# Layer 1 three segments behind layer 0 instead of four, in a two-layer recurrent-memory transformer

## The chip, the core and the metric

The kernel runs on one core of a Trainium2 chip. TensorE (PE, with its weight loads PEld) multiplies matrices into PSUM; VectorE (DVE) and ScalarE (ACT) read PSUM and do the element-wise work; GpSimd (POOL) works on SBUF only and issues some DMAs; SyncE (SP) issues most of them. The metric is the device time of one execution in microseconds, the median of the runs shown. The profile is one further execution.

## The reference

```python
def A(x, mem0, Wq, Wk, Wv, Wo):                 # x: 2048 x 512, 32 heads of 128
    mem = mem0                                  # 8 rows
    for s in range(64):                         # segments of 32 rows
        h = concat([mem, x[32*s:32*s+32]])      # 40 rows
        q, k, v = h @ Wq, h @ Wk, h @ Wv        # per head
        p = softmax(mask(q @ k.T * scale))
        o = (p @ v) @ Wo                        # summed over the heads
        mem = o[:8]; out[s] = o[8:]
B = lambda x: relu(x @ w1) @ w2                 # 512 -> 1376 -> 512
x = x + A(layernorm(x), ...);  x = x + B(layernorm(x))      # layer 0
x = x + A(layernorm(x), ...);  x = x + B(layernorm(x))      # layer 1, same weights
```

The recurrence is the memory: segment s needs the eight memory rows that segment s-1 has made. All weights stay in SBUF. Operands are bf16, sums and residual rows f32.

## The kernel before

**Steps.** Step k does segment k of layer 0 and, at the same time, segment k-4 of layer 1 (`DELTA = 4`; the segment of layer 1 done in step s has the name s). Steps 0 to 3 have only layer 0, steps 4 to 63 both, steps 64 to 67 only layer 1. Where both run, the 40 rows of each lie side by side in `HT` and are the 80 moving columns of one matmul per block of weights. A step's TensorE queue is written out by hand (as are those of VectorE, SP and GpSimd; ScalarE's is ordered by a scheduler when the program is built):

1. `qk` (L580 to L615): queries and keys of heads 0 to 15 into `qp`, evicted by ScalarE (`QT`) and VectorE (`KT`); then some filler; then `scores` into the banks `sp`. VectorE and ScalarE do the softmax of this half (`exponentials`, `softmax`; its products are on GpSimd, the last one of a step on VectorE), and a DMA transpose makes `PT0`.
2. The same for heads 16 to 31. The first dense product (`dense_h`, tile `hp`) lies ahead of the second scores. Filler follows while the softmax of the second half runs, then `transpose_p` on TensorE (tile `tp`), `weighted_v` (tile `pv`) and the copies `outputs`.
3. The hand-over of the memory: `output_mem` (tile `wo`), ScalarE's copy `wm`, the selection matmuls `mt`, the copies into `HT` and `HTm`, `memory_values` (tile `vm`). Then the next step.

**Filler** is what no step waits for: outputs of the previous step's token rows (`output_x`, tile `wox`), the dense layer (`dense_h`, `dense_y`), values of layer 0's later segments (`values0`, tile `vp`) and of layer 1's next segment (`values1`, tile `v`). Values go to DRAM and come back in a later step into `Vs`. `values1(k + 1)` fills the two waits of the hand-over, 16 matmuls each.

**Riding.** `output_mem` has stationary blocks of 32 columns: 16 are the memory rows of the two layers, 16 are spare. Token rows of segments k % 4 == 0 ride in the spare columns of two steps, layer 0's in steps k and k+1, layer 1's in k+2 and k+3 (`ride0`, `ride1`, `output_ride`, `add_ride`). The others go through `output_x` one step later, both layers' 64 rows as one block of width 64 (L373, two side by side in the array).

**Residual rows.** `residual(d)` is a 128 x 512 tile for two steps; a step has 64 rows, layer 0's 32 and layer 1's 32. Rows of d are normalized in step k = d + 2 (`prepare`, `normalize_step`; VectorE, with one `pow` on GpSimd), transposed by a DMA (`transpose_step`), used by `dense_h(k - 2)` and by `values1`, and summed by `dense_y` (L543, width 64) and `add_dense`. Layer 0's finished rows are copied to the place where layer 1 will add to them (L566).

**PSUM.** `ps_c` has three buffers (queries, keys, `mt`, `vm`), `ps_fill` two (`hp`, `v`, `vp`, `xp` and two of the `pv`), `ps_wo` one (`wo`, `wox`, a `vp`), and two banks hold the scores and, in turn, the dense sums.

Of the kernel before, what the change touches and what calls it, by code (L numbers as in the profile page):

```python
# [16 lines left out]
LN_EPS = 1e-5  # L17
DELTA = 4
# [4 lines left out]
def kernel(  # L23
# [23 lines left out]
    assert NSEG % 4 == 0 and DELTA == 4  # L47
    LAST = NSEG + DELTA - 1
    NXT = NSEG // 4
    NC4 = Dm // 128  # L50
    NFC = (Dff + 127) // 128
# [23 lines left out]
    def ride0(k):  # L75
        return has0(k) and k % 4 == 0

    def ride1(s):
        return has1(s) and s % 4 == 0 and s + DELTA <= LAST

    def place1(s):
        if ride1(s):
            return s + 4, 32
        if s >= LAST - 1:
            return LAST - 1, 32 * (s - LAST + 1)
        return s, (0 if s % 4 == 0 else 32)
# [6 lines left out]
    def base(d):  # L93
        return 64 * (d % 2)

    def span(d):
        offs = ([0] if has0(d) else []) + [o for o, _ in slots_of.get(d, [])]
        return base(d) + min(offs), base(d) + max(offs) + 32
# [11 lines left out]
    R_tiles = {}  # L110

    def residual(d):
        i = d // 2
        if i not in R_tiles:
            R_tiles[i] = wk.tile([128, Dm], F32, tag=f"R{i % 2}", bufs=3 - i % 2, name="R")
        return R_tiles[i]

    def load_x(k):
        r = base(k)
        nc.gpsimd.dma_start(out=residual(k)[r:r + SEG, :], in_=A_x[0, SEG * k:SEG * k + SEG, :])  # L120
# [41 lines left out]
    mhalf_t = const.tile([128, 1], F32)  # L162
# [30 lines left out]
    stats_all = const.tile([128, 6], F32)  # L193
    nc.vector.bn_stats(out=stats_all[:], in_=XN[:])
# [20 lines left out]
    xT0, xnT_tiles, hT_tiles, vd0, vd1, vmds, wm_tiles, wo_tiles, xp_tiles, vp_tiles, obs = {}, {}, {}, {}, {}, {}, {}, {}, {}, {}, {}  # L215

    def stat_tail(stats, of=""):
        mom = wk.tile([128, 3], F32, tag="ln_mv" + of, bufs=2 - len(of), name="mv")
# [3 lines left out]
        nc.gpsimd.tensor_tensor(out=rstd, in0=rstd, in1=mhalf_t[:], op=ALU.pow)  # L222
        return mv, rstd
# [11 lines left out]
    def moments_x(n):  # L235
        return stat_tail(stats_x(n), "x")
# [17 lines left out]
    def norm_parts(k):  # L254
        parts = []
        d = k - 2
        if 0 <= d <= LAST:
            parts.append((nc.vector, residual(d)) + span(d))
        if has1(k + 1):
            g = k + 1 - DELTA  # L260
            parts.append((nc.vector, residual(g), base(g), base(g) + SEG))
        return parts

    def moments(k, later):
        for _, R, lo, hi in norm_parts(k)[1:] if later else norm_parts(k)[:1]:
            nc.vector.bn_stats(out=stats_all[lo:hi, :], in_=R[lo:hi, :])

    norm_rows = {}

    def normalize_step(k):  # L270
        mom = stat_tail(stats_all) if norm_parts(k) else None
        masks(*layers(k))
        def rows():
            for eng, R, lo, hi in norm_parts(k):
                normalize(eng, XN, R, mom, lo, hi)


        if len(layers(k)) == 1 or k == DELTA:
            norm_rows[k] = rows
        else:  # L280
            rows()
# [4 lines left out]
    def transpose_step(k):  # L286
        if not norm_parts(k):
            return
        t = xnT_tiles[k] = wk.tile([128, NC4, 128], BF, tag="xnT", bufs=1, name="xnT")
        if k <= LAST:  # L290
            nc.sync.dma_start_transpose(out=t[:], in_=XN[:])
        else:
            tp = transpose_pe(XN)
            nc.scalar.copy(out=t[:], in_=tp[:])
# [3 lines left out]
    evict_behind = []  # L298

    def values0(p, n, lo=0, hi=NC4, pool=None, stage=None, late=False):  # L300
# [15 lines left out]
        if late and evict_behind:  # L316
            with tc.issue_after(evict_behind[0]):
                nc.scalar.copy(out=vst, in_=vp[:])
        else:
            nc.scalar.copy(out=vst, in_=vp[:])  # L320
# [15 lines left out]
    def values_second(ii, stage):  # L336
        if ii == 0:
            vd0[0] = dram.tile([2, 4, 32, 512], BF, tag="vd_second", bufs=1, name="vd_second")
        values_tile(xT0[0][:, :, SEG:2 * SEG], ii, vd0[0], stage)

    def values1(s, ii):
# [4 lines left out]
        r = base(s - DELTA)  # L346
        values_tile(xnT_tiles[s - 1][:, :, r:r + SEG], ii, vd1[s])

    def values_tile(tokens, ii, vd, stage=None):
        vp = ps_fill.tile([128, 512], F32, tag="fill", name="v1")  # L350
        for c4 in range(NC4):
            for j in range(4):
                n = 4 * ii + j
                nc.tensor.matmul(vp[32 * j:32 * j + 32, :], lhsT=tokens[:, c4, :],  # L354
# [3 lines left out]
        nc.scalar.copy(out=vst, in_=vp[:])  # L358
# [4 lines left out]
    def ox_span(k):  # L363
        offs = ([0] if has0(k) and not ride0(k) else [])
        if has1(k) and not ride1(k):
            offs.append(place1(k)[1])
        r = base(place1(k)[0] if k == LAST else k)
        return (r + min(offs), r + max(offs) + 32) if offs else None

    def halves(out, lhsT, rhs, start, stop):  # L370
        nr = lhsT.shape[-1]
        for j in range(2):
            nc.tensor.matmul(out[64 * j:64 * j + nr, 0:256], lhsT=lhsT, rhs=rhs[:, 256 * j:256 * j + 256],  # L373
                             start=start, stop=stop, tile_position=(0, 64 * j))

    def add_halves(dst, in0, half_sums):
        nr = in0.shape[0]
        for j in range(2):
            nc.vector.tensor_tensor(out=dst[:, 256 * j:256 * j + 256], in0=in0[:, 256 * j:256 * j + 256],
                                    in1=half_sums[64 * j:64 * j + nr, 0:256], op=ALU.add)  # L380

    def output_x(k, lo, hi):
        if not 0 <= k <= LAST or ox_span(k) is None:
            return
        r0, r1 = [x % 64 for x in (ox_span(k)[0], ox_span(k)[1] - 1)]
        r1 += 1
        if lo == 0:
            pool, tag = (ps_wo, "wo") if k < LAST else (ps_c, "c")
            wo_tiles[k] = pool.tile([128, Dm], F32, tag=tag, name="wox")
        for h in range(lo, hi):  # L390
            if r1 - r0 == 64:
                halves(wo_tiles[k], OTx[:, h, r0:r1], Wo_sb[:, h, :], h == 0, h == H - 1)
            elif by_heads(k):
                for j in range(2):
                    q = 32 * (2 * (h % 2) + j)
                    nc.tensor.matmul(wo_tiles[k][q:q + 32, 0:256], lhsT=OTx[:, h, r0:r1],  # L396
                                     rhs=Wo_sb[:, h, 256 * j:256 * j + 256], start=(h < 2), stop=(h >= H - 2),
                                     tile_position=(0, q))
            else:
                for j in range(4):  # L400
                    nc.tensor.matmul(wo_tiles[k][32 * j:32 * j + 32, 0:128], lhsT=OTx[:, h, r0:r1],
                                     rhs=Wo_sb[:, h, 128 * j:128 * j + 128], start=(h == 0), stop=(h == H - 1),
                                     tile_position=(0, 32 * j))

    def by_heads(k):
        return k == LAST or len(layers(k + 1)) == 1

    def add_last(k, part):

        r = 64 * (LAST - k)  # L410
        R = residual(LAST - 1)
        nc.vector.tensor_tensor(out=R[r:r + 64, 0:256], in0=R[r:r + 64, 0:256],
                                in1=wo_tiles[k][64 * part:64 * part + 64, 0:256], op=ALU.add)
# [3 lines left out]
    def last_rows(k, eng):  # L417
# [3 lines left out]
        R = residual(LAST - 1)  # L421
# [6 lines left out]
        nc.vector.bn_stats(out=stats[:, 0, :], in_=R[r:r + 64, 0:256])  # L428
# [5 lines left out]
        nc.gpsimd.tensor_tensor(out=rstd, in0=rstd, in1=mhalf_t[r:r + 64, :], op=ALU.pow)  # L434
        eng.tensor_scalar(out=XN[r:r + 64, 0:256], in0=R[r:r + 64, 0:256], scalar1=mv[:, 0:1], scalar2=rstd[:, 0:1],  # L435
                          op0=ALU.subtract, op1=ALU.mult)

    def turn_last(k, t, copy):
        r = 64 * (LAST - k)
        c = SEG * (LAST - k)  # L440
# [4 lines left out]
        copy(out=t[:, :, c:c + SEG].rearrange("p (j b) t -> p b j t", j=2),  # L445
             in_=tp[:].rearrange("p b (j t) -> p b j t", j=2))

    def add_output(k, part=None):
        if not 0 <= k <= LAST or ox_span(k) is None:
            return  # L450
        r0, r1 = ox_span(k)
        R = residual(k)
        if by_heads(k) and r1 - r0 == 32:
            for q in range(4):
                if part in (None, q // 2):
                    cs = slice(256 * (q % 2), 256 * (q % 2) + 256)
                    nc.vector.tensor_tensor(out=R[r0:r1, cs], in0=R[r0:r1, cs],
                                            in1=wo_tiles[k][32 * q:32 * q + 32, 0:256], op=ALU.add)
        elif part == 1:
            return  # L460
# [20 lines left out]
    def output_ride(k):  # L481
        if ride_rows(k) is None:
            return
# [667 lines left out]
```

## Time and profile before

| what | value |
|---|---|
| median of 3 runs | 1582.27 us (1580.9 to 1583.86) |
| span of the profiled execution | 1580.0 us |
| PE busy | 1548.6 us, 98%, 42866 matmuls |
| PEld busy | 1286.3 us, 81% |
| DVE busy | 1277.3 us, 81% |
| ACT busy | 734.7 us, 47% |
| POOL busy | 349.8 us, 22% |
| step 1 begins (first `qp` matmul) | 51.20 us |
| step 3 begins | 91.97 us |
| step 4, the first with both layers, begins | 111.66 us |
| step 64, the first with layer 1 alone, begins | 1495.70 us |

Matmuls are pipelined, and four or two of them run side by side where their stationary blocks are narrow, so the mean duration of one (200 ns for L591) is not what it costs; the distance from one group's start to the next one's is. The queue share of the page says that TensorE works nearly always; which group it works on, and what would stand behind it, is read from its timeline.

### The profile page before, as it was taken

The numbers are of one execution on the slowest core, as the hardware profiler recorded it, in microseconds if no ns is written. First come the engines' busy times: TensorE is split into PE (matmuls) and PEld (weight loads), VectorE is DVE, ScalarE is ACT, GpSimd is POOL, SyncE is SP. The second block draws the span as 40 slices with busy tenths as digits, with TensorE's granted clock in tenths as the row PEclk, the third lists the DMA queues.
The fourth block names the chain that finished last, engine by engine and source line by source line (L and its number), as shares of the span: only waits on it lengthen the run. The fifth ranks groups of instructions, "written<-read, shape, count | busy, mean of one in ns | idle before, by whom it ended". The sixth has DMA issues, their size and how long they took to land. (4 is left out here: it accounts for less than half of the span.)

```text
span 1580.0 us, 95139 instructions
## 1 busy us (share of the span) xinstructions
PE 1548.6 (98%) x42866; PEld 1286.3 (81%) x42866; DVE 1277.3 (81%) x3300; ACT 734.7 (47%) x1762; POOL 349.8 (22%) x670
## 2 busy tenths in 40 slices
PE   5899999999999999999999999999999999999998
PEld 3677888888888888888888888988888898888876
DVE  3578888888888888888888888888888888887866
ACT  3435445454544545454454545445454544545433
POOL 2012122222222222222122222212222221222110
PEclk9999999999999999999999999999999999999999
DMA  9734432434353244434433343443443344333331
GB/s 369 246 77 76 87 84 78 81 92 79 78 92 84 78 82 94 80 76 91 84 80 80 99 80 76 88 84 79 77 99 77 72 87 80 82 74 95 75 69 41
DMA packets 222021, 146.26 MB, mean 93 GB/s; under 512 B 123464, under 2 KB 215984, under 8 KB 221616
## 3 DMA queue, kind: packets, MB, share of 16 engines
q1 hardware_dynamic: 218448, 135.96, 38.8%
q8 instruction: 336, 5.51, 1.5%
q0 software_dynamic: 3072, 4.20, 1.1%
q14 instruction: 69, 0.57, 0.1%
q10 hardware_dynamic: 96, 0.03, 0.0%
HBM read 65.41 MB, written 45.35 MB: 70 GB/s over the span
## 5 line engine op out<-in xcount | busy, mean ns | idle before, releaser
L597 ACT CAST QT<-qp 128x480 bf16<-128x480 f32 (+3 forms) x408 | 201.5, 494 | 433.4 <-PE qp L591 433.1
L591 PE MATMUL qp<-HT,Wq_sb 128*128 128x80 bf16 (+1 forms) x8704 | 371.3, 200 | 3.2 <-POOL HT L786 1.2
L591 PEld LDWEIGHTS <-Wq_sb 128*128 128x128 bf16 x8704 | 325.9, 100 | 35.2 <-issue 27.5
L591 PE MATMUL qp<-HT,Wk_sb 128*128 128x80 bf16 (+1 forms) x8704 | 347.3, 199 | 1.7 <-issue 1.3
L591 PEld LDWEIGHTS <-Wk_sb 128*128 128x128 bf16 x8704 | 319.5, 100 | 2.6 <-issue 1.6
L664 POOL TENSOR_TENSOR P_sb<-es,sm 128x320 bf16<-128x320 f32 x185 | 130.8, 721 | 714.8 <-ACT QT L597 299.4
L599 DVE CAST KT<-qp 128x480 bf16<-128x480 f32 (+3 forms) x408 | 220.3, 565 | 36.3 <-PE qp L591 32.9
L643 DVE TENSOR_REDUCE mx<-sp 128x8 f32<-128x320 f32 x256 | 115.1, 487 | 133.1 <-PE sp L625 130.9
L373 PE MATMUL wox<-Wo_sb,OTx 128*64 128x256 bf16 x2880 | 173.6, 273 | 0.0
L373 PEld LDWEIGHTS <-OTx 128*64 128x64 bf16 x2880 | 150.2, 110 | 2.9
L649 ACT ACTIVATE es<-es 128x320 f32<-128x320 f32 x256 | 109.5, 468 | 61.9 <-DVE es L647 61.0
L797 PE MATMUL vm<-Wv_sb,HTm 128*32 128x512 bf16 x2176 | 129.4, 379 | 1.8 <-DVE KT L599 1.0
L354 PE MATMUL v<-Wv_sb,xnT 128*32 128x512 bf16 x2048 | 128.8, 378 | 0.0
L633 PE MATMUL wo<-Wo_sb,OTm 128*32 128x512 bf16 x2144 | 128.6, 380 | 0.0
L659 DVE TENSOR_REDUCE sm<-es 128x8 f32<-128x320 f32 x256 | 117.4, 459 | 13.5 <-ACT es L649 5.0
L617 DVE CAST sp<-maskb 128x320 f32<-128x320 bf16 x256 | 118.3, 483 | 0.0
L647 DVE TENSOR_TENSOR es<-sp,mx 128x320 f32<-128x320 f32 x256 | 113.6, 482 | 1.5
L543 PE MATMUL sp<-w_sb,hT 128*64 128x256 bf16 (+4 forms) x1452 | 103.9, 276 | 0.4 <-issue 0.4
L522 PE MATMUL hp<-xnT,w_sb 128*128 128x64 bf16 (+1 forms) x2948 | 98.5, 192 | 0.9 <-issue 0.5
L801 ACT CAST VmS<-vm 128x512 bf16<-128x512 f32 x134 | 78.5, 586 | 44.4 <-PE vm L797 42.5
L222 POOL TENSOR_TENSOR mv<-mv,mhalf_t 128x1 f32<-128x1 f32 x82 | 45.8, 558 | 224.6 <-DVE mv L221 218.9
L797 PEld LDWEIGHTS <-HTm 128*32 128x32 bf16 x2176 | 54.7, 97 | 48.8 <-issue 3.1
(125 smaller groups left out, 2088.5 us busy)
## 6 DMA issues: line engine op xcount, KB each, us to landing
Vs<-vd SPq DMA_DIRECT2D x96, 256.0 KB
vd<-vst SPq DMA_DIRECT2D x181, 128.0 KB
vmd<-VmS SPq DMA_DIRECT2D x134, 128.0 KB
Vs<-vmd SPq DMA_DIRECT2D x254, 32.0 KB
Vs<-vmd SPq DMA_DIRECT2D x60, 128.0 KB
Wq_sb<-in_A_Wq_dram SPq DMA_DIRECT2D x2, 2048.0 KB
Wk_sb<-in_A_Wk_dram SPq DMA_DIRECT2D x2, 2048.0 KB
Wv_sb<-in_A_Wv_dram SPq DMA_DIRECT2D x2, 2048.0 KB
```

The source lines that it names most:

```text
L354: nc.tensor.matmul(vp[32 * j:32 * j + 32, :], lhsT=tokens[:, c4, :], rhs=Wv_sb[:, c4, n * 512:(n + 1) * 512], start=(c4 == 0), stop=(c4 == ...
L373: nc.tensor.matmul(out[64 * j:64 * j + nr, 0:256], lhsT=lhsT, rhs=rhs[:, 256 * j:256 * j + 256], start=start, stop=stop, tile_position=(0, ...
L591: nc.tensor.matmul(qp[:, hi, 0:ncol], lhsT=W_sb[:, c4, h * Dh:(h + 1) * Dh], rhs=HT[:, c4, a_lo:a_hi, :], start=(c4 == 0), stop=(c4 == NC4 ...
L597: nc.scalar.copy(out=dst[:, 0:nh, a_lo * L:a_hi * L], in_=qp[:, 0:nh, 0:ncol])
L599: nc.vector.tensor_copy(out=dst[:, 0:nh, a_lo * L:a_hi * L], in_=qp[:, 0:nh, 0:ncol])
L617: nc.vector.tensor_copy(out=sp_tiles[a], in_=maskb2)
L633: nc.tensor.matmul(wo[32 * j:32 * j + 32, :], lhsT=OTm[:, h, n, 2 * M * c:2 * M * c + 4 * M], rhs=Wo_sb[:, h, :], start=(h < 4), stop=(h > ...
L643: nc.vector.tensor_reduce(out=mxs[a][:], in_=sp, axis=AX.X, op=ALU.max)
L647: nc.vector.tensor_tensor(out=es[:], in0=sp, in1=mxs[a][:].unsqueeze(2).to_broadcast([128, 8, L]), op=ALU.subtract)
L659: nc.vector.tensor_reduce(out=sm[:], in_=es[:], axis=AX.X, op=ALU.add)
L664: eng.tensor_tensor(out=P, in0=es[:], in1=sm[:].unsqueeze(2).to_broadcast([128, 8, L]), op=ALU.mult)
L797: nc.tensor.matmul(vp[32 * j:32 * j + 32, :], lhsT=HTm[:, c4, :], rhs=Wv_sb[:, c4, n * 512:(n + 1) * 512], start=(c4 == 0), stop=(c4 == NC ...
```

## The change

Layer 1 runs three segments behind layer 0. Steps 0 to 2 are layer 0 alone, 3 to 63 both, 64 to 66 layer 1 alone: 67 steps in place of 68. For this, layer 0's rows have to be finished a step earlier:

- Layer 0's outputs are made in their own step, in the hand-over (`output_own`, called in `new_memory` and `make_room`), where `values1` stood; `values1(k + 1)` moves ahead of them, into the second half's filler.
- Layer 0 doesn't ride. Every second segment of layer 1 does (`s % 2 == 0`); the others are `output_late`, 32 rows in the step behind. Every output block has width 32, four side by side.
- Residual rows lie by column halves: 64 partitions by 256 columns for a segment, so that each add or statistic takes half as many columns on twice the partitions. The halves' statistics are exchanged by four small copies, and `dense_y` has blocks of width 32. Loads and stores of such rows are two DMAs in place of one.
- The dense layer of d is done in step d + 1 in place of d + 2. The rows are normalized behind the first key copy of the step (`norm_rows`, `behind[0]`).
- Layer 0's value groups: 0, 1 or 2 in odd steps (48 over the 29 odd steps from 5 to 61), in place of 3 or 4 in every fourth.

```diff
-DELTA = 4
+DELTA = 3
...
     def ride1(s):
-        return has1(s) and s % 4 == 0 and s + DELTA <= LAST
+        return has1(s) and s % 2 == 0 and s + 4 <= LAST
...
+    def output_rows(t, a, lo, hi):
+        for h in range(lo, hi):
+            for j in range(2):
+                q = 32 * (2 * (h % 2) + j)
+                nc.tensor.matmul(t[q:q + 32, 0:HALF], lhsT=OTx[:, h, SEG * a:SEG * a + SEG],
+                                 rhs=Wo_sb[:, h, HALF * j:HALF * j + HALF], start=(h < 2), stop=(h >= H - 2),
+                                 tile_position=(0, q))
+    def output_own(k, lo, hi):
+        if lo == 0:
+            own_tiles[k] = ps_fill.tile([128, Dm], F32, tag="fill", name="own")
+        output_rows(own_tiles[k], 0, lo, hi)
...
     def dense_y
-            for j in range(2):
+            for q in range(2 * slots(d)):
+                o, j = divmod(q, 2)
-                nc.tensor.matmul(sp_banks[bank][64 * j:64 * j + n, 0:w], lhsT=hT_tiles[d][0:fs, fc, 0:n],
+                nc.tensor.matmul(sp_banks[1][32 * q:32 * q + 32, 0:w], lhsT=hT_tiles[d][0:fs, fc, SEG * o:SEG * o + SEG],
...
     def new_memory(k, cont, wo):
         nc.scalar.copy(out=wm_sb[:], in_=wo[:])
-        values1(k + 1, 0)
+        if has0(k):
+            output_own(k, 0, H // 2)
+        else:
+            values1(k + 1, 0)
...
     def prepare(k):
         moments(k, True)
+        add_own(k - 1)
         add_ride(k - 1)
         moments(k, False)
         normalize_step(k)
+    def make_room(k):
+        if has0(k):
+            output_own(k, H // 2, H)
+        else:
+            values1(k + 1, 1)
+        output_ride(k)
...
     def step(k):
+        first = 4 if k == LAST else 8 if single else 10
+        output_late(k, 0, first)
+        value_group(k, 0, 0, 2)
...
+        if k != LAST and not (single and has0(k)):
+            dense_h(d)
         with tc.high_priority(offset=PRIO):
             scores(qks, act)
             softmax(1, act, by_pe)
+        evict_behind.append(last_exp[0].ins)
+        value_group(k, 0, 2, NC4)
+        if single and has0(k):
+            value_group(k, 1, late=True)
+            dense_h(d)
...
+        if has0(k) and has1(k + 1):
+            values1(k + 1, 0)
+        output_late(k, second, H)
+        if not (single and has0(k)):
+            value_group(k, 1, late=True)
+        value_group(k, 2, late=True)
+        if has0(k) and has1(k + 1):
+            values1(k + 1, 1, late=True)
+        evict_behind.clear()
+            dense_y(d, 0, f_mid)
+            add_late(k)
```

An eviction with `late` is issued by ScalarE behind the last exponential of the step; one without has the place that the scheduler gives it.

More of the change, by code (lines that the diff above doesn't have):

```diff
@@ L315, in values0 @@
         vst = wk.tile([128, 512], BF, tag="vst", bufs=5, name="vst")[:] if stage is None else stage
[L316 to L320, printed above, removed]
+        evict(vst, vp[:], late)
         nc.sync.dma_start(out=vd0[p][n // 2].rearrange("j t e -> (j t) e"), in_=vst)
@@ L357, in values_tile @@
         vst = wk.tile([128, 512], BF, tag="vst", bufs=5, name="vst")[:] if stage is None else stage
-        nc.scalar.copy(out=vst, in_=vp[:])
+        evict(vst, vp[:], late)
         nc.sync.dma_start(out=vd[ii].rearrange("j t e -> (j t) e"), in_=vst)
[L363 to L368, printed above, removed]
```

521 lines of the change are left out of this document (200 added, 321 removed).

## The prediction

> **What bounds the kernel now.** I read the page's shares first (PE busy 98% of the span, DVE 81%, ACT 47%), then the busy time of each engine step by step. A step begins where the first `qp` matmul of a segment starts. The columns are: the stretch, its length, then busy time and instructions of PE, PEld, DVE, ACT, POOL, granted clock, DMA share, GB/s.
>
> ```profile
> 91.97:111.66 19.69, 19.08 (x582) 14.69 (x579) 14.70 (x38) 7.55 (x19) 3.71 (x8) 1.00 0.29 74
> 780.93:803.46 22.53, 22.53 (x611) 17.85 (x607) 19.20 (x51) 12.06 (x28) 5.66 (x11) 1.00 0.52 100
> 826.54:849.62 23.08, 23.08 (x650) 19.81 (x647) 19.56 (x51) 10.59 (x25) 5.34 (x10) 1.00 0.37 82
> ```
>
> A step with both layers lasts 23.08 us (22.53 in those that carry three groups of layer 0's values instead of outputs), and TensorE is busy throughout at full clock. A step with one layer lasts 19.69, nearly as long. The 60 two-layer steps run from 111.66 to 1495.70, 1384.0 us; four one-layer steps stand ahead and four (84.3 us) behind. So I price TensorE's queue from the start of one group to the start of the next, in the timeline of one step (start, us, count at the end):
>
> ```profile
> 836.89 1.45 PE L522 MATMUL hp<-xnT,w_sb 128*128 128x64 bf16 x44
> 838.27 0.57 PE L625 MATMUL sp<-KT,QT 128*40 128x40 bf16 x32
> 838.69 3.12 PE L373 MATMUL wox<-Wo_sb,OTx 128*64 128x256 bf16 x54
> 841.64 1.18 PE L543 MATMUL sp<-w_sb,hT 128*64 128x320 bf16 x18
> 842.65 0.45 PE L675 MATMUL tp<-ident,P_sb 128*64 128x80 bf16 x16
> 842.93 0.39 PE L543 MATMUL sp<-w_sb,hT 128*64 128x256 bf16 x4
> ...
> 844.16 1.91 PE L633 MATMUL wo<-Wo_sb,OTm 128*32 128x512 bf16 x32
> 845.90 1.04 PE L354 MATMUL v<-Wv_sb,xnT 128*32 128x512 bf16 x16
> 846.76 0.27 PE L857 MATMUL mt<-sel,wm 128*32 128x16 bf16 x16
> 846.87 1.03 PE L354 MATMUL v<-Wv_sb,xnT 128*32 128x512 bf16 x16
> 847.73 0.23 PE L488 MATMUL xp<-wm,sel 128*32 128x128 bf16 x4
> 847.79 1.90 PE L797 MATMUL vm<-Wv_sb,HTm 128*32 128x512 bf16 x32
> 849.62 0.57 PE L591 MATMUL qp<-HT,Wq_sb 128*128 128x80 bf16 x11
> ```
>
> The number behind the star is the width of the stationary block. `wo` and `vm` are the same 32 matmuls of width 32 on 512 columns. `wo`, followed by width 32, takes 845.90 - 844.16 = 1.74; `vm`, followed by width 128, takes 1.83. So **a change of width costs about 0.1 us**. The same in one-layer steps, where the dense rows are 32 wide:
>
> ```profile
> 102.40 1.06 PE L396 MATMUL wox<-Wo_sb,OTx 128*32 128x256 bf16 x32
> 103.28 1.18 PE L543 MATMUL sp<-w_sb,hT 128*32 128x320 bf16 x18
> 104.58 0.48 PE L675 MATMUL tp<-ident,P_sb 128*64 128x80 bf16 x16
> 104.99 0.40 PE L543 MATMUL sp<-w_sb,hT 128*32 128x256 bf16 x4
> ```
>
> Here `tp` to `sp` (64 to 32) takes 0.41, against 0.28 above (64 to 64). `wox` x32 of width 32 takes 0.88, and x16 followed by width 64 takes 0.55 (99.70 to 100.25), which is half of 0.88 plus 0.11.
>
> Last, the wait that the filler in mid-step has to cover. The score matmuls start at 838.27, and VectorE ends the last probabilities at 842.48:
>
> ```profile
> 838.69 0.89 DVE L643 TENSOR_REDUCE mx<-sp 128x8 f32<-128x320 f32 x2 [1.26 <-PE sp L625]
> ...
> 841.86 0.62 DVE L664 TENSOR_TENSOR P_sb<-es,sm 128x320 bf16<-128x320 f32 x1
> ```
>
> That is 4.21 after the scores began. With 0.1 for the hand-over `tp` could start at 4.31, and TensorE arrives at 4.38 (842.65). The kernel has no slack there.
>
> **The change, part by part.**
>
> *One step fewer.* The built program has 61 two-layer steps (3 to 63) and 67 in all. By forms this removes 512 `qp` matmuls of 40 columns at about 26 ns (13.4 us) and adds 256 of 80 columns at 36 (9.2); 32 `wo` and 32 `vm` go (3.6), and one two-layer step's `sp` and `pv` replace two one-layer ones' (1.2). That is 9 us less matmul work. Matmuls of width 64 on 256 columns become twice as many of width 32, four side by side: `wox` x32 at 0.88 is 27.5 ns each, half the 54.6 of L373, so this alone is worth nothing.
>
> *An even step (layer 1's outputs late).* Base 23.08.
> - Outputs: own 32 + 32 at 0.88 each, late 20 (5 fours: 0.55 + 0.11) and 44 (1.21): 3.63, against 0.57 + 2.95 before: +0.11. Layer 1's two value groups (0.86 each) only move from the step's end to its middle.
> - Dense sums: 36 + 8 of width 32 instead of 18 + 4 of width 64: +0.02 in length, +0.10 into `tp`, +0.10 behind it.
> - Scores (width 64) are now followed by width 32: +0.09 (0.50 for the 32 at 123.52, 0.42 here).
>
> Sum 23.50. `tp` is reached 0.51 + 0.86 + 1.21 + 0.86 + 1.13 = 4.57 after the scores. But ScalarE's order, as built, puts the eviction of the first value group (0.59) between its two exponentials. The group is finished about 1.6 after the scores, the first exponential starts at 1.74, so the second starts at 2.63 instead of 2.14, and VectorE's second sum, which had 0.2 to spare, comes 0.29 late: `tp` at 4.60. Wait 0.03, say 0.05: **23.55**, 30 times.
>
> *An odd step with two groups of layer 0's values.* No late outputs. Half a group in place of `wox` x10: 0.46 for 0.57. In the middle: half group 0.55, values 0.97, group 0.98, values 0.86 (three more changes of width, 64 to 32 and back) = 3.37 for 2.95. With 0.06 more in own and dense lengths and 0.2 at `tp`: 23.65. The second value group needs the PSUM buffer of the first (two `fill` buffers), whose eviction ScalarE puts behind both exponentials: 2.57 to 3.16 after the scores, while TensorE is there at 2.93. Wait 0.3: **23.95**, 19 times.
>
> *An odd step with one group.* Middle 2.28, so 22.56, and `tp` is reached 0.42 + 2.28 + 1.13 = 3.83 after the scores, 0.5 before it can start: **23.06**, 10 times, and step 3 likewise. Step 63 has no group: 21.6 and a wait of 1.0, **22.6**.
>
> *Sum of the two-layer steps.* 706.5 + 455.1 + 230.6 + 23.1 + 22.6 = 1437.9. Before, 12 x 22.53 + 48 x 23.1 = 1379.2, and the rest of its 1384.0 (4.9) was pauses marked "issue"; I add 5: **1443**.
>
> *Start.* Step 3 began at 91.97. Own outputs of steps 0 to 2 add 5.3; a second dense stage 2.7; values for step 3, 1.7; step 2's `wox` goes (2.0). Five gaps at the memory hand-overs (0.69, 0.47, 0.73, 0.34, 0.42) are filled by the own outputs: -2.6. The first dense stage is now in step 1, reached at about 64.4, and its weights are issued at 60.2: 1.41 MB at the 305 GB/s of 61 to 66 land near 66.3, the second 1.4 MB near 70. Waits of 2 and 0.6, less the 0.6 that TensorE spent there for the probabilities. Step 3 begins at **99** (97 to 103).
>
> *End.* The last three steps took 64.2; with the dense changes of width **64.8**.
>
> *What lies beside other work.* VectorE's chain ahead of the next step gains own sums (2 x 0.42) and four copies (0.16), loses two of the four 0.28 ride sums and half of each statistic (0.42 for 0.69), and the normalisation goes behind the first key copy. That copy starts 2.2 after the step's start, by these rows, against 2.64 now; the later ones 0.1 later, with 0.5 to spare before the scores. The normalised rows are ready at 3.7 instead of 2.6, so SP issues the transpose 1.1 later (1.2 us, then four loads of memory rows, needed only at 16.7); `hp`, which needs it, is at 10.3. Its landing shows in no row; the larger `PT` transpose took 5.84, so I bound this one by 0 and 5.84 from the issue and take no wait. A wait per us of lateness would cost 61 us. POOL has a second load to issue (0.59) where it sits idle 3.8, SP a second store (0.34) where it idles 0.1 to 1 between its issues; the two stores of layer 1's values (0.4 each) leave the step's end for its middle, where SP has nothing to issue from 839.6 to 848; own sums for VectorE's `OTx` copies: ready at 18.9 and 19.2 in the step, used at 19.7 and 20.7. I take 0.
>
> **Sum:** 99 + 1443 + 64.8 = 1606.8, against the profiled 1580.0: +27. The median of the runs is 2.3 above the profile, so I say **1609**.
>
> Changes of width make the sign: four more in an even step, five or three in an odd one, 251 in all, 24 us at 0.095. [...]
>
> **Rivals.**
> - *The changes of width are free and the fillers cover the chain* (faster). Then only the matmuls count: 24 and about 16 of waits less, 1569. For it: the trace has no idle time in these steps. Against it: each pair of rows above. The point from which it decides is 27 us saved of these 40, so a change of width at nearly 0. Chance 0.05.
> - *The changes cost as shown, but the waits vanish* (two PSUM buffers and ScalarE's order do not bind): 1593. For it: each wait is a difference of two sums, 0.03 to 0.9. Chance 0.13.
> - *The transpose comes late.* `hp` is 10.3 after the step's start and the issue at 3.9 to 5.1; it decides from a landing 5.2 after the issue ends. At 5.84 the price is 0.64 x 61 = 39: 1648. Against it: half of `PT`'s bytes. Chance 0.07.
> - *The forecast*, 0.75: own range 1598 to 1620.
>
> The range goes from 1593 (no waits) to 1625 (the waits twice as long): 0.85 of the chance. What can be told from no change is about 0.2%, 3 us. Faster 0.05, same 0.02, slower 0.93.
>
> **What would show it.** Two-layer steps of 23.5 (even) and 23.95 or 23.06 (odd); `sp` to `tp` gaps on PE ended by DVE's `P_sb` in odd steps with one group, and `v` ended by ScalarE's `vst` in those with two; a gap before the first `hp` near 64; a pause of 0.1 at each change of width. Wrong would be two-layer steps at or under 23.1, or idle time before `hp` in all of them.

## The result, and the profile after

| kernel | median | runs | span of the profiled execution |
|---|---|---|---|
| before | 1582.47 us | 1580.9 to 1583.86 (4) | 1580.0 us |
| changed | 1618.21 us | 1617.2 to 1621.24 (4) | 1616.0 us |

The ratio is 1.0229, 95% interval 1.0215 to 1.0244: slower by 36 us, of which 27 were forecast. An undisturbed step, here and below, is one of the shortest length that steps of its kind take again and again. The page of the changed kernel (span, shares of the engines, the queues of GpSimd's transfers and of the instruction fetches):

```profile
span 1616.0 us, 103053 instructions
...
PE 1568.8 (97%) x46705; PEld 1273.1 (79%) x46706; DVE 1229.6 (76%) x3463; ACT 728.4 (45%) x1708; POOL 365.4 (23%) x733
...
q0 software_dynamic: 6144, 4.20, 1.8%
q8 instruction: 366, 6.00, 1.6%
```

VectorE's busy time fell by 48 us and ScalarE's by 6. TensorE's rose by 20, with 3839 more matmuls, and TensorE is the engine that sets the time (busy for 97% of the span; 85% of the chain that ended last is its). The three kinds of two-layer step, in the busy time of each engine by stretch (length, then PE, PEld, DVE, ACT, POOL, clock, DMA share, GB/s):

```profile
741.11:764.66 23.55, 23.55 (x737) 19.71 (x733) 19.09 (x54) 10.54 (x25) 5.55 (x11) 1.00 0.32 76
764.66:788.56 23.90, 23.75 (x688) 18.84 (x685) 18.31 (x53) 11.69 (x27) 5.55 (x11) 1.00 0.45 91
812.10:835.24 23.14, 22.65 (x680) 18.40 (x677) 18.85 (x55) 11.05 (x26) 5.89 (x12) 1.00 0.37 83
```

An even step, an odd one with two groups of layer 0's values, an odd one with one: 23.55, 23.90 and 23.14, where 23.55, 23.95 and 23.06 were forecast. The middle of the even step on TensorE:

```profile
752.94 0.58 PE L573 MATMUL sp<-KT,QT 128*40 128x40 bf16 x32
753.45 1.05 PE L357 MATMUL v<-Wv_sb,xnT 128*32 128x512 bf16 x16
754.32 1.37 PE L371 MATMUL wox<-Wo_sb,OTx 128*32 128x256 bf16 x44
755.52 1.04 PE L357 MATMUL v<-Wv_sb,xnT 128*32 128x512 bf16 x16
756.39 1.18 PE L498 MATMUL sp<-w_sb,hT 128*32 128x320 bf16 x36
757.53 0.48 PE L623 MATMUL tp<-ident,P_sb 128*64 128x80 bf16 x16
757.94 0.40 PE L498 MATMUL sp<-w_sb,hT 128*32 128x256 bf16 x8
```

No idle time; `tp` to `sp` is 0.41, as in the old one-layer steps, where it was 0.28 in the old two-layer ones. In an odd step with one group the probabilities come too late for `tp`; the profile names the last thing VectorE did ahead of `tp` (L219), which ended 0.1 behind the probabilities:

```profile
826.45 1.18 PE L498 MATMUL sp<-w_sb,hT 128*32 128x320 bf16 x36
828.12 0.48 PE L623 MATMUL tp<-ident,P_sb 128*64 128x80 bf16 x16 [0.49 <-DVE mv L219]
```

The waits of all two-layer steps (101.19 to 1546.64; total us, times, longest) are few. These are the four largest of eight; the view leaves out idle times up to 0.15 us, and so 12 of the 19 waits ahead of `v` for its buffer:

```profile
PE tp L623 <- DVE P_sb L612: 3.6, 6, 1.2
PE tp L623 <- DVE mv L219: 2.4, 5, 0.5
PE qp L539 <- issue: 1.9, 4, 0.7
PE v L357 <- ACT vst L306: 1.1, 7, 0.2
```

From the starts of the steps the 36 us divide so:

| part | before | changed | difference | forecast, changed |
|---|---|---|---|---|
| up to step 3 | 91.97 | 101.19 | +9.2 | 99 |
| steps with both layers (before: with steps 3 and 64) | 1423.8 | 1445.5 | +21.7 | 1443 |
| the last three steps and the end | 64.2 | 69.4 | +5.2 | 64.8 |

The 1423.8 is 19.69 + 1384.0 + 84.3 - 64.2, so that both columns hold the same work: 61 steps of 23.70 in place of 60 of 23.07 and two of 20.

### The profile page after: what moved, and what is told of

It reads as the page before. It is cut to its first block, busy times and chain, and to the rows that moved or that the text cites. A ratio compares the mean times of both kernels' runs of the same rounds, so it can differ in the third digit from the quotient of the medians.

```text
span 1616.0 us, 103053 instructions
## 1 busy us (share of the span) xinstructions
PE 1568.8 (97%) x46705; PEld 1273.1 (79%) x46706; DVE 1229.6 (76%) x3463; ACT 728.4 (45%) x1708; POOL 365.4 (23%) x733
## 3 DMA queue, kind: packets, MB, share of 16 engines
q0 software_dynamic: 6144, 4.20, 1.8%
## 4 chain that ended last, share of the span: by engine, by line
PE 85%; DVE 3%; issue 2%; ACT 2%; POOL 0%; POOLq 0%; ACTq 0%
PE qp L539 36%; PE wo L581 7%; PE vm L724 7%; PE own L371 7%; PE hp L482 5%; PE v L357 5%; PE sp L498 4%; PE wox L371 4%; PE sp L573 3%; PE pv L649 3%; PE tp L623 2%; DVE es L595 1%; PE vp L318 1%; ACT es L597 1%; ACT vst L306 1%
## 5 line engine op out<-in xcount | busy, mean ns | idle before, releaser
L539 PE MATMUL qp<-HT,Wq_sb 128*128 128x80 bf16 (+1 forms) x8576 | 367.3, 200 | 1.8 <-POOL HT L710 1.2
L371 PEld LDWEIGHTS <-OTx 128*32 128x32 bf16 x6272 | 161.3, 96 | 26.0 <-issue 2.9
L371 PE MATMUL own<-Wo_sb,OTx 128*32 128x256 bf16 x4096 | 131.5, 272 | 0.5 <-issue 0.3
L728 ACT CAST VmS<-vm 128x512 bf16<-128x512 f32 x132 | 77.2, 585 | 103.5 <-PE vm L724 103.5
L276 POOL TENSOR_TENSOR mv<-mv,mhalf_t 128x2 f32<-128x2 f32 (+1 forms) x66 | 46.5, 705 | 295.8 <-DVE mv L275 261.5
L498 PE MATMUL sp<-w_sb,hT 128*32 128x256 bf16 (+1 forms) x2772 | 104.8, 276 | 0.8 <-DMA w_sb<-in_B_w_dram 0.5
L482 PEld LDWEIGHTS <-w_sb 128*128 128x128 bf16 x2948 | 90.3, 98 | 7.2 <-DMA w_sb<-in_B_w_dram 5.6
```

The source lines that it names most:

```text
L371: nc.tensor.matmul(t[q:q + 32, 0:HALF], lhsT=OTx[:, h, SEG * a:SEG * a + SEG], rhs=Wo_sb[:, h, HALF * j:HALF * j + HALF], start=(h < 2), s ...
L482: nc.tensor.matmul(hp[:, fc - f0, 0:n].rearrange("p (s t) -> p s t", s=ns), lhsT=w1_sb[:, c4, u:u + 128], rhs=cols(c4), start=(c4 == 0), s ...
L498: nc.tensor.matmul(sp_banks[1][32 * q:32 * q + 32, 0:w], lhsT=hT_tiles[d][0:fs, fc, SEG * o:SEG * o + SEG], rhs=w2_flat[0:fs, fc * Dm + HA ...
L539: nc.tensor.matmul(qp[:, hi, 0:ncol], lhsT=W_sb[:, c4, h * Dh:(h + 1) * Dh], rhs=HT[:, c4, a_lo:a_hi, :], start=(c4 == 0), stop=(c4 == NC4 ...
```

## The experiments

All ratios are to the kernel before.

**1. Only the dense sums narrow, in the kernel before.**

```diff
-            for j in range(2):
+            for q in range(2 * (n // 32)):
+                j, o = divmod(q, n // 32)
+                p = 64 * j + 32 * o
-                nc.tensor.matmul(sp_banks[bank][64 * j:64 * j + n, 0:w], lhsT=hT_tiles[d][0:fs, fc, 0:n],
+                nc.tensor.matmul(sp_banks[bank][p:p + 32, 0:w], lhsT=hT_tiles[d][0:fs, fc, 32 * o:32 * o + 32],
...
-                                 tile_position=(0, 64 * j))
+                                 tile_position=(0, p))
```

> The kernel before, with the dense sums of a two-layer step as four matmuls of width 32 side by side for each chunk and matrix instead of two of width 64 (44 matmuls instead of 22, the same sums). Everything else stays. Theory (a change of the stationary block's width costs about 0.095 us, the number of matmuls nothing): three more changes in each of 60 two-layer steps (64 to 32 ahead of the sums, 32 to 64 into the transposes, 64 to 32 behind them), 0.02 for the length of the sums: steps of 23.4 instead of 23.08, 18 us in all, a median near 1601; the gap from the start of the transposes to the start of the sums behind them grows from 0.28 to about 0.41. Rival (the change of width is free, and it is waits that cost time in the changed kernel): 1582 to 1584, steps of 23.1. Second rival (twice as many matmuls cost more by themselves): the sums x36 take clearly more than the 1.01 of x18, and the gap at the transposes stays 0.28.

Measured: 1602.33 us, ratio 1.0124 (1.0108 to 1.0139), +19.9 us. Steps of 23.43, and 22.80 in those with three value groups (22.53 before). Its timeline in step 35:

```profile
847.58 3.12 PE L373 MATMUL wox<-Wo_sb,OTx 128*64 128x256 bf16 x54
850.62 1.19 PE L543 MATMUL sp<-w_sb,hT 128*32 128x320 bf16 x36
851.75 0.48 PE L675 MATMUL tp<-ident,P_sb 128*64 128x80 bf16 x16
852.16 0.40 PE L543 MATMUL sp<-w_sb,hT 128*32 128x256 bf16 x8
```

`wox` x54 reaches the next group in 3.04 (2.95 where width 64 follows), the sums take 1.13 with the change into `tp` (1.01), `tp` 0.41 (0.28): 0.09, 0.12 and 0.13, in a kernel whose order and waits are the old ones. (23.43 - 23.08 - 0.02) / 3 is 0.11 for each change. Doubling the matmuls cost next to nothing by itself here: less 0.11 for the change into `tp`, the 36 sums take 1.02, and the 18 took 1.01.

**2. Layer 1's outputs narrow as well, in the kernel before.** To the edit above comes:

```diff
-        for j in range(2):
-            nc.tensor.matmul(out[64 * j:64 * j + nr, 0:256], lhsT=lhsT, rhs=rhs[:, 256 * j:256 * j + 256],
-                             start=start, stop=stop, tile_position=(0, 64 * j))
+        for q in range(4):
+            j, o = divmod(q, 2)
+            nc.tensor.matmul(out[32 * q:32 * q + 32, 0:256], lhsT=lhsT[:, 32 * o:32 * o + 32],
+                             rhs=rhs[:, 256 * j:256 * j + 256],
+                             start=start, stop=stop, tile_position=(0, 32 * q))
```

> As the first run, and layer 1's outputs too are four matmuls of width 32 side by side instead of two of width 64, still in layer 0's and layer 1's common tile and at their old places; four segments of distance, transposes, loads and waits as before the change. Theory (changes of width): in the steps that carry outputs a fourth change (width 32 ahead of and behind the first outputs and behind the scores, none any more between outputs and sums): 23.5, as in an even step of the changed kernel; in the 12 steps with three value groups as the first run, 22.85; in all 23 to 24 us, a median near 1606, which is most of the changed kernel's loss without any of its order. Rival (the loss comes from the new order: waits and late transposes): 1582 to 1586. A kernel at 1600 to 1603 would say that the outputs' changes cost less than those of the sums.

Measured: 1630.49 us, ratio 1.0302 (1.0282 to 1.0323), +48 us: twice what was expected. Undisturbed steps last 23.51 to 23.55, just as expected and just as the changed kernel's even ones. But 29 of the 44 two-layer steps that carry these outputs are longer, by up to 2 us. One of them, and the four largest of the nine waits of the two-layer steps (113.08 to 1545.76):

```profile
791.47 1.93 PE L374 MATMUL wox<-Wo_sb,OTx 128*32 128x256 bf16 x64
794.43 1.38 PE L374 MATMUL wox<-Wo_sb,OTx 128*32 128x256 bf16 x44 [1.02 <-issue]
```

```profile
PE wo L635 <- issue: 4.4, 7, 0.8
PE qp L593 <- issue: 4.0, 10, 0.7
PE wox L374 <- issue: 2.5, 5, 1.0
PE pv L703 <- issue: 2.3, 5, 0.9
```

TensorE stops in the middle of a row of equal matmuls whose data has long been there. The page counts 369 transfers on the instruction queue for 47,065 matmuls (336 for 42,866 before, 366 for 46,705 in the changed kernel): one fetch of 16,384 bytes for 127.5 matmuls. Pauses that follow each other directly are 125 to 128 matmuls apart, and each of the 49 in these steps ends 1.0 to 2.1 us behind the end of such a fetch. From the trace's DMA records and TensorE's matmul count, around the two pauses of step 34:

```
fetch from 839.48 to 841.36 us;   pause ends at 842.88, matmul 23,793
fetch from 844.37 to 845.41 us;   pause ends at 847.02, matmul 23,920
```

The profile puts the second of them down to `OTx`; its place, 127 matmuls behind the first and 1.6 us behind a fetch, is that of the others. That TensorE was out of instructions there is my reading: the records show the fetches and the stops, not what joins them. The fastest tenth of all stretches of 128 matmuls took at most 3.30 us here, 3.61 in the changed kernel, 3.93 in the one before. Taken as 12 undisturbed steps of 22.80 and 48 of 23.52, the two-layer steps would take 1402.6 us, 23.4 more than before without pauses (1379.2), which is the price of the changes; they took 1432.7, so that pauses are some 30 us.

**3 and 4. Changes of width added to the changed kernel, with a control.** Two matmuls of 16 columns among the second half of the own outputs, of width 64 or of width 32; their result goes to columns that nothing reads.

```diff
-        output_rows(own_tiles[k], 0, lo, hi)
+        t = own_tiles[k]
+        cuts = (lo, hi) if lo == 0 else (lo, 20, 28, hi)
+        for c0, c1 in zip(cuts, cuts[1:]):
+            if c0 > lo:
+                nc.tensor.matmul(t[0:64, 256:272], lhsT=ident[:, 0:64], rhs=ident[:, 0:16], start=True, stop=True,
+                                 skip_group_check=True, tile_position=(0, 0))
+            output_rows(t, 0, c0, c1)
```

> The changed kernel with two added matmuls of 16 columns and width 64 among the second half of each segment's own outputs (after heads 20 and 28; their result goes to unused columns), 64 steps. Theory (changes of width): four more changes a step, 64 x 4 x 0.095 = 24 us, and the matmuls themselves 1 to 3: a median near 1644. Rival (a change of width is free; it was the number of groups or waits): as the next run, within 2 us.

> The control of the run before: the same two matmuls of 16 columns at the same places, but of width 32, so that no width changes. Theory (changes of width): 1 to 4 us over the changed kernel, 1619 to 1622; the difference to the run before, 24 us, is the price of 256 changes of width. Rival (any added matmul between the others costs as much): as the run before.

Measured: 1651.74 us (ratio 1.0439, 1.0421 to 1.0456) with width 64, 1624.80 (1.0269, 1.0254 to 1.0284) with width 32. The second half of the own outputs in each, width 64 first:

```profile
827.39 0.39 PE L371 MATMUL own<-Wo_sb,OTx 128*32 128x256 bf16 x8
827.71 0.20 PE L402 MATMUL own<-ident 128*64 128x16 bf16 x1
827.83 0.62 PE L371 MATMUL own<-Wo_sb,OTx 128*32 128x256 bf16 x16
```

```profile
814.76 0.39 PE L371 MATMUL own<-Wo_sb,OTx 128*32 128x256 bf16 x8
814.98 0.17 PE L402 MATMUL own<-ident 128*32 128x16 bf16 x1
814.99 0.71 PE L371 MATMUL own<-Wo_sb,OTx 128*32 128x256 bf16 x19
```

The eight matmuls ahead last 0.32 or 0.22 from start to start, the small one 0.12 or 0.01: a tenth of a microsecond each way, and nothing where the width stays. Undisturbed even steps are 24.03 and 23.58 (23.55 without), odd ones 24.39 and 23.94: 0.45 for four changes, **0.11 each**. The medians differ by 26.9 us for 256 changes, 0.105 each. The control cost 6.6 us, more than the 1 to 4 expected: 0.04 a step is 2.6, and steps that are longer than undisturbed ones make up the rest; waits marked issue rose from 3.0 to 4.6 us in the two-layer steps.

**5. The kernel of run 2 with the same changes of width, but wide in the middle: fewer instructions, more changes.** In the kernel of run 2, `halves` takes the width from a flag:

```diff
-        for q in range(4):
-            j, o = divmod(q, 2)
+        n = 32 if narrow else 64
+        for q in range(128 // n):
+            j, o = divmod(q, 64 // n)
...
-                halves(wo_tiles[k], OTx[:, h, r0:r1], Wo_sb[:, h, :], h == 0, h == H - 1)
+                halves(wo_tiles[k], OTx[:, h, r0:r1], Wo_sb[:, h, :], h == 0, h == H - 1, h < 7 or h >= H - 2)
```

> The second run with 23 of layer 1's 27 heads in the long stretch at width 64 again; the four heads at its two ends and the five early heads stay at width 32. Per step that is 46 matmuls fewer and two changes of width more. Theory (code supply: the pauses marked issue, 24 us in the second run, come where 128 matmuls, which is one fetch of 16 KB of instructions, take less than about 3.8 us; they follow the number of instructions): most pauses go, 2 to 6 us of them stay, and two changes in 48 steps cost 9 us: 1606 + 9 + 2 to 6, a median of 1614 to 1621, faster than the second run in spite of more changes of width; undisturbed steps 23.7. Rival (the pauses are part of the price of narrow matmuls or of the changes): 1636 to 1645, undisturbed steps of 23.7 and as many pauses or more.

Measured: 1615.23 us, ratio 1.0213 (1.0198 to 1.0228): 15 us faster than run 2 with two more changes a step. Undisturbed steps are 23.75, so these two cost 0.12 each. The waits of its two-layer steps, whole list:

```profile
PE qp L593 <- issue: 1.1, 3, 0.4
PE wox L403 <- issue: 0.7, 1, 0.7
```

So the pauses of run 2 don't go with the changes of width: with two more of them a step, the two-layer steps took some 3 us more than undisturbed ones, and in run 2 some 30. Run 5 has fewer matmuls in that stretch and, by the same edit, fewer narrow blocks; against the blocks speaks the changed kernel, where every output block is 32 wide and pauses are 7.5 us. The 3.8 us of the expectation is an estimate between the 3.61 of the changed kernel and the 3.93 of the one before; no run shows a limit there.

**6. One load of the residual rows per segment.**

```diff
-        for j in range(2):
-            nc.gpsimd.dma_start(out=residual(k)[SEG * j:SEG * j + SEG, :],
-                                in_=A_x[0, SEG * k:SEG * k + SEG, HALF * j:HALF * j + HALF])
+        nc.gpsimd.dma_start(out=residual(k)[0:2 * SEG, :],
+                            in_=A_x[0, SEG * k:SEG * k + SEG, :].rearrange("t (j c) -> j t c", j=2))
```

> The changed kernel with each segment's rows loaded by one GpSimd transfer, as before the change, and not by two (64 transfers, not 128, of the same bytes). Theory (GpSimd's last drain grows by about 0.08 us with each transfer that it issued, and the changed kernel ends with it): the drain takes 5.9 us and not 11.1, the span ends about 4 us earlier, where the last stores land; a median near 1614.5; the steps stay. Rival (the drain waits for something else, or is as long as it is in any case): 1617 to 1619, a drain of 10 to 11 us.

Measured: 1629.95 us, ratio 1.0304 (1.0286 to 1.0321), 12 us slower than the changed kernel. The end came sooner, near what was expected: the last step with what follows it went from 29.24 to 25.76. But GpSimd's last drain, which the engine's own instruction records in the trace show, went from 11.13 to 1.99 us and not to 5.9, so it does not go by the number of transfers. And this transfer was cut differently, as the page's queue line shows (packets, MB, share):

```profile
q0 software_dynamic: 33792, 4.31, 2.6%
```

528 packets for each segment, not 96. Undisturbed steps stayed 23.55, 23.90 and 23.15, yet the two-layer steps together took 1457.8 us, 12 more, in pauses that again end 0.9 to 2.2 us behind instruction fetches. That the small packets (33,792, and 6,144 in the changed kernel) delay the fetches is a guess; no run shows where they meet.

**7. The dense weights ahead.** In step 1 `load_dense()` goes from behind the first softmax to right behind `load_values`.

> The changed kernel with the dense weights' loads of step 1 issued by SyncE ahead of the memory values' stores and loads and of the first transpose. Theory (the first dense stage waits 5.1 us for these weights because SyncE issues them 1.6 us later than before the change, behind the new transpose): the wait falls to 1 to 2.5 us, step 3 begins at 98 to 99 and not at 101.2, a median of 1615 to 1616. Rival (the transfers share their bandwidth, so the time is only moved to the memory values that then land later): step 3 begins at 100.5 to 101.5, a median of 1617 to 1619.

Measured: 1620.44 us, ratio 1.0243 (1.0226 to 1.0259): no gain. Step 3 began at 99.88 instead of 101.19, between the two expectations. The wait ahead of `hp` fell, and another came ahead of it, in the second scores:

```profile
65.38 0.26 PE L573 MATMUL sp<-KT,QT 128*40 128x40 bf16 x3 [1.99 <-issue]
...
69.95 1.25 PE L482 MATMUL hp<-xnT,w_sb 128*128 128x32 bf16 x44 [1.20 <-DMA xnT<-XN]
```

`hp` now waits for the transpose, which stands behind the weights on SyncE's queue. The 1.99 ends 1.49 us behind a fetch of instructions, as the pauses of run 2 do (1.0 to 2.1). The fetch ran from 62.76 to 63.89, beside the weights' transfers, and began when TensorE had started 978 matmuls; the same fetch of the changed kernel began behind 880. Of the 1.3 us at step 3 nothing is left at the end: the two-layer steps took 1447.4 us instead of 1445.5, and between the changed kernel and run 8, whose step 1 ran at another clock without an edit there, step 3 moved by as much (1.3 us; see the start, below).

**8. Two orders in the odd steps.**

```diff
+        if not (single and has0(k)):
+            value_group(k, 1)
         if has0(k) and has1(k + 1):
             values1(k + 1, 0)
         output_late(k, second, H)
-        if not (single and has0(k)):
-            value_group(k, 1, late=True)
...
-        f_mid = 9
+        f_mid = NFC if k % 2 and not single and len(values_at(k)) < 2 else 9
```

> The changed kernel with two orders changed. In odd steps with two groups of layer 0's values, the second follows the first and its eviction is ScalarE's before the second exponential, not the last: two changes of width fewer, and no wait for the fill buffer. In odd steps with one group, all dense sums go ahead of the transposes: one change fewer, 0.3 us more of cover for the 0.48 that TensorE waits for the probabilities. Theory (0.095 us for each change, waits as read from the changed kernel's trace): the first kind 23.6 to 23.7, not 23.90 (19 times), the second kind 22.75 to 22.9, not 23.13 (10 times); together -7 to -9 us, a median near 1610. Rival (the wait moves: a later exponential or the transposed probabilities hold TensorE instead): 23.9 and 23.1 as they were, a median of 1617 to 1620.

Measured: 1608.60 us, ratio 1.0172 (1.0153 to 1.0191), 9.6 us faster than the changed kernel. Odd steps with two groups last 23.50 instead of 23.90, those with one 22.95 instead of 23.14. An odd step with two groups:

```profile
772.42 1.47 PE L318 MATMUL vp<-Wv_sb,xT 128*64 128x512 bf16 x12
773.82 1.97 PE L357 MATMUL v<-Wv_sb,xnT 128*32 128x512 bf16 x32
775.60 1.20 PE L498 MATMUL sp<-w_sb,hT 128*32 128x320 bf16 x36
776.72 0.48 PE L623 MATMUL tp<-ident,P_sb 128*64 128x80 bf16 x16
```

No wait for the `fill` buffer (0.22), and two changes fewer (0.18 for both, by what is left of the 0.40). The order of the groups in this step is worth nearly as much as the wait (0.18 and 0.22).

**9. The residual rows through SyncE.** Loaded as they are, a step earlier, and cast by GpSimd:

```diff
+        for j in range(2):
+            rows = residual(k)[SEG * j:SEG * j + SEG, :]
+            if k < 2:
+                nc.gpsimd.dma_start(out=rows, in_=A_x[0, SEG * k:SEG * k + SEG, HALF * j:HALF * j + HALF])
+        if k >= 2:
+            nc.gpsimd.tensor_copy(out=residual(k)[0:2 * SEG, :], in_=xr_tiles.pop(k)[:])
+        if k >= 1 and has0(k + 1):
+            xr = xr_tiles[k + 1] = wk.tile([2 * SEG, HALF], BF, tag="xr", bufs=2, name="xr")
+            for j in range(2):
+                nc.sync.dma_start(out=xr[SEG * j:SEG * j + SEG, :],
+                                  in_=A_x[0, SEG * (k + 1):SEG * (k + 2), HALF * j:HALF * j + HALF])
```

> The changed kernel with the rows of segments 2 to 63 loaded by SyncE as they are (bf16) into a tile of their own, one step earlier, and cast into the residual tile by GpSimd: 4 GpSimd transfers in all instead of 128, and no packets split. Theory (the drain goes with what GpSimd issued, and nothing else waits for it): the drain is under 1 us, the span ends with the last stores, 3.5 to 4.5 us earlier, two-layer steps stay 23.55, 23.90 and 23.13, a median of 1613 to 1615. Second part, from the sixth run: the pauses marked issue, which grew by some 10 us with 33,792 software packets, are at most as many as with 6,144, which may give 0 to 4 us more. Rival (two more issues on SyncE a step delay its transposes): waits ahead of hp or behind the transposes in every step, a median above 1618.

Measured: 1618.09 us, ratio 1.023 (1.0216 to 1.0244): the changed kernel's time. The drain is 1.00 us and the last step takes 26.12 instead of 29.24, a little less than was expected. The 3.1 us came back elsewhere: the first `hp` waits 6.34 instead of 5.13 (more issues stand ahead of the weights on SyncE), step 3 begins 1.6 later, and step 65 has a pause of 1.26. Two-layer steps took 1446.4 us, 1.0 more; so no harm of 6,144 software packets shows beside 192.

**10. Three edits together** (8, 9 and 7).

> The changed kernel with three edits together: the value groups and dense sums of the eighth run, the loads of the ninth, and the dense weights' loads of the seventh. Theory: -9.5 for the first (as measured), -3.5 to -4.5 for the second, -1.3 for the third, pauses equal within 3: a median of 1602 to 1606. It still has two changes of width around the transposes and narrow outputs in every step, which is why it stays 20 us behind the kernel before. Rival (the edits take the same idle time): 1607 to 1610.

Measured: 1610.45 us, ratio 1.0174 (1.0158 to 1.019): at the upper end of the rival's range, no better than run 8 alone. Against run 8, step 3 begins 1.0 later (103.5) and the two-layer steps take 2.9 more (1437.4 for 1434.6), which is more than the 1.9 that the end gives. No version of the changed kernel that was run comes within 26 us of the one before.

## Why the prediction was right, and where it missed

**The sign and its cause were right.** Changes of width of the stationary block were to make the loss, and runs 1, 3 and 5 show that they do, each by itself: 0.11 us for a change in runs 1 and 3, 0.12 in run 5. Where the width stays, a small matmul took 0.01 (run 4). Runs 3 and 4 give the price by the step: two added matmuls of another width make an undisturbed step 0.48 to 0.49 us longer, the same two without a change of width 0.03 to 0.04. What TensorE does in this time, no run shows. The prediction took 0.095 from pairs of groups, so its 24 us for 251 changes are nearer 28. Run 2 puts these changes into the old order, with four segments of distance, and gets the changed kernel's even step of 23.5. So narrow blocks make this price without the new order and without three segments of distance. Why the changed kernel has them is read from its layout and order, not from a run: residual rows by column halves keep the two halves of one layer's row side by side on 64 partitions, so that a block of `dense_y` holds one layer's rows, and layer 0's outputs are made a step ahead of layer 1's. Whether three segments of distance could be had with wide dense sums, no run shows.

**The two-layer steps.** 30 x 23.545 + 19 x 23.90 + 10 x 23.135, with 22.83 and 23.37 for steps 3 and 63, is 1438.0 without pauses; the prediction's was 1437.9. That the sums agree to 0.1 is luck, because inside small errors cancel: an even step's wait of 0.05 is not there (`tp` starts 4.59 behind the scores, 4.57 to 4.60 were forecast), and four changes at 0.11 instead of 0.095 fill the place. The wait for the `fill` buffer costs 0.22 instead of 0.3 (0.53 from the last `vp` to `v`, 0.31 where nothing waits). The wait in an odd step with one group is 0.49 (0.5 forecast). Step 63 is 0.8 longer than forecast: its wait for the probabilities is 1.16 (1.0), and it has one ahead of its first scores (0.31 idle) that the prediction did not have; step 3 is 0.3 shorter. Pauses are 7.5 us and not 5, which is the whole miss of this part: the step that failed is "I add 5", which carried the old kernel's pauses over although the matmuls rose by 9% and 128 of them stand closer (3.61 us for the fastest tenth, 3.93 before).

**The start, 2.2 us late.** The step that failed is the landing of the first dense weights: "its weights are issued at 60.2". SyncE in the changed kernel, then in the one before (start, us to issue):

```profile
58.32 1.30 SPq L292 DMA_TRANSPOSE xnT<-XN  x1
59.73 1.99 SPq L734 DMA_DIRECT2D Vs<-vmd  x2
61.77 0.41 SPq L155 DMA_DIRECT2D w_sb<-in_B_w_dram  x1
```

```profile
59.04 1.11 SPq L807 DMA_DIRECT2D Vs<-vmd  x2
60.20 0.40 SPq L157 DMA_DIRECT2D w_sb<-in_B_w_dram  x1
```

The dense stage that moved into step 1 brought its transpose with it, and that stands ahead of the weights; the two issues behind it take 1.99 us instead of 1.11. The weights are issued at 61.77, and TensorE waits 5.1 us, not 2:

```profile
69.72 1.36 PE L482 MATMUL hp<-xnT,w_sb 128*128 128x32 bf16 x44 [5.13 <-DMA w_sb<-in_B_w_dram]
...
73.43 1.19 PE L498 MATMUL sp<-w_sb,hT 128*32 128x320 bf16 x18 [0.51 <-DMA w_sb<-in_B_w_dram]
```

The prediction had counted that transpose in steady steps and not here. The later issue is 1.6 of the 3.4 us by which `hp` starts behind the forecast landing of 66.3. The rest lies in the transfer: from 61 to 66 the core's DMAs moved 200 GB/s, not the 305 that the prediction took from the kernel before. How little the issue alone decides shows in run 8, which leaves step 1 as it is: there the weights are issued 0.8 later (62.61), and `hp` starts 0.2 earlier (69.47). Runs 7 and 9 show how tight the queue is at this place: with the weights ahead, `hp` waits 1.20 for its transpose and the scores 1.99 (run 7); with more issues ahead of the weights, `hp` waits 6.34 instead of 5.13 (run 9).

The prediction also had nothing for the clock behind this wait. In the changed kernel the granted clock is 0.5 from 69.5 to 72.9 (in the kernel before, which has no such wait, it is 1.00 there), and each pair of side-by-side `vp` matmuls behind `hp` takes 0.43 us in place of 0.22 (run 7, at full clock). The wait for the second weights comes behind that and hides the loss. In run 8 the clock stays at 0.5 to 76.7, the work from the end of that second wait to step 2 takes 9.68 us instead of 8.21, and step 3 begins at 102.49. So two profiles can differ by some 1.3 us at step 3 without an edit that bears on it.

**The end, 4.6 us late.** The last three steps were taken over with "the dense changes of width". Two things were missed. The one-layer steps have the wait for the probabilities too, 0.59 in steps 64 and 65:

```profile
1559.94 0.48 PE L623 MATMUL tp<-ident,P_sb 128*64 128x80 bf16 x16 [0.59 <-DVE P_sb L612]
```

And "POOL has a second load to issue (0.59) where it sits idle" was true of the steps, but the loads have a second price at the end of the program: GpSimd's drain of 11.13 us, from 1604.12 to 1615.25, while the last store's packets had ended at 1611.4. Before it lasted 5.90, from 1570.97, and ended ahead of the last store (1578.3). Runs 6 and 9 shorten it and the last step by 3.5 and 3.1 us.

**The rivals.** Free changes of width: run 3 against its control, run 4, excludes it. Vanishing waits (1593): they are there, 0.22 to 0.5 in odd steps. The late transpose: no `hp` in a two-layer step waits.

## What to carry to other kernels

Count the changes of the stationary block's width in TensorE's queue as instructions of about 0.11 us (runs 1, 3 and 5: 0.11 to 0.12); a layout that makes blocks narrow paid this at its borders with wide ones, even though the narrow matmuls themselves were as fast side by side (36 of width 32 in 1.02 us, 18 of width 64 in 1.01). Count instructions too where short matmuls stand in long rows: where the fastest tenth of all stretches of 128 took 3.30 us (run 2), pauses were 30 us; at 3.61 and 3.93 they were 7.5 and 4.9. And when a stage moves to an earlier step, write down the whole order of the queue that feeds it in that step, with every transfer that now stands ahead (here the weights were issued 1.6 us later) or is under way at the same time.

## What the runs showed of the hardware that was not expected

- *TensorE stopped in rows of matmuls whose data was there, and the stops ended behind instruction fetches.* The kernels have one fetch of 16,384 bytes for 127.5 matmuls and as many weight loads (336 for 42,866 of each before, 366 for 46,705 in the changed kernel). Each of the 49 pauses in the two-layer steps of run 2 ends 1.0 to 2.1 us behind the end of a fetch. In run 2, with 108 matmuls of 27 ns in a row, pauses took 30 us; with 46 fewer matmuls a step (run 5) the two-layer steps took some 3 us more than undisturbed ones. How far ahead TensorE fetches, no run here shows.
- *GpSimd ends with a drain, of 1.00 to 11.13 us in these kernels.* From the instruction records of the trace:

```
kernel    GpSimd transfers   packets   drain
before          64            3,072     5.90 us
changed        128            6,144    11.13 us
run 6           64           33,792     1.99 us
run 9            4              192     1.00 us
```

  The first two would be 0.09 us for a transfer; run 6, with 64 transfers and 1.99 us, excludes that this is the rule. What the drain counts stays open.
